# Four f tiles instead of six in the first phase of a fused attention and feed-forward kernel, with all later weights converted beside the attention

## The chip, the cores and the metric

The kernel runs on one core of one Trainium2 chip. The metric is the device time of one execution in microseconds (us). Engines are called as the profile calls them: PE is TensorE, DVE is VectorE, ACT is ScalarE, POOL is GpSimd, and SP is SyncE, whose queue issues nearly all DMAs.

## What is computed

Block-causal attention over 8 batches of 8 heads, 576 positions and 64 channels each, and on its output, as 4608 tokens of 512 channels, a feed-forward layer of width 2048 with a leaky activation:

```python
scores = scale * np.matmul(q, k.transpose(0, 1, 3, 2))        # (8, 8, 576, 576)
mask = block_i >= block_j                                     # blocks of 64
scores = np.where(mask, scores, -1000000000.0)
attn = np.exp(scores - np.max(scores, axis=-1, keepdims=True))
attn = attn / (np.sum(attn, axis=-1, keepdims=True) + 1e-09)
out = np.matmul(attn, v)
...
x = np.ascontiguousarray(attn_out.transpose(0, 2, 1, 3)).reshape(B * S, H * D)
h = x @ w_in                                                  # (4608, 512) x (512, 2048)
g = np.maximum(h, 0.0) + alpha * np.minimum(h, 0.0)
return (g @ w_out).astype(np.float32)                         # (2048, 512)
```

q, k and v are float32; the two weight matrices come as 64-bit floats, so that a half of an f tile's weights (its part of `w_in` or of `w_out`, 512 values per partition) arrives as 1024 words of 32 bits, and the kernel makes float32 of it.

## The kernel before

**Precision.** Products of float32 values are made of pairs: a value is split into a high part (rounded to the matmul's format by ACT) and a low part (the difference, by POOL or DVE; `split`, L526). A product is then three matmuls: high by high, high by low, low by high.

**Attention.** Two heads make a pair; there are 32 pairs, four to a batch. `prep` (L771) loads q, k and v of a pair, splits q and k, and moves the parts through 10 DMAs into the tiles `Q` and `K`. `query_tile` (L863) makes scores of 128 queries on PE (L890, L952), the negative maximum on DVE (L897, L903), the exponential with its sum on ACT (L906), sums and reciprocal on DVE (L910, L912), the scaling on POOL (L914), transposes on PE (L922, L978), and copies them from PSUM to `PTF` on ACT or DVE (L996, L998). `values` (L1000) multiplies with v (L1022); ACT copies the result into `xT` (L1026), a ring of two batches, and `spill` (L1032) stores each batch to `xd` in DRAM.

**Feed-forward, first phase.** The 2048 columns are 16 f tiles of 128. Tiles 0 to `FA` - 1 (six) are computed beside the attention, in 18 chunks of 256 tokens (`chunk_a`, L739): `split_x` makes `xh` and `xl`, `ffn1` (L615) is 12 matmuls of 256 columns per f tile (L623), `activate` (L631) works on ACT (L634, L640), DVE (L636) and POOL (L643), and `ffn2` (L647) adds three matmuls of 512 columns per f tile and 128 tokens (L660). The sum over these tiles goes to `part` in DRAM. The chunks fill PE between the attention's products.

**Feed-forward, later phase.** Once attention has ended its buffers are freed (`end_attention`, L1074), and the other ten f tiles are taken two by two over nine chunks of 512 tokens, with Strassen's scheme in Winograd's form for the first product: seven products of half size (`pair1`, L690; six matmuls of 256 columns each, L701) instead of eight. For that, sums of quarters of the weights (`ws`, L545) and of the tokens (`xt`, L545) are made and split (`w`, `X`, L529). DVE adds up the products (L710, L714). `store_out` (L1109) adds `part` and stores.

**Weights.** `to_f32` (L493) converts a half: one load of 512 KB on SP's queue into one of two `raw` buffers, then DVE (L507), ACT (L510) and DVE four times (L512, L516, L519, L522), with two PSUM banks. The 12 halves of the first phase are converted at the start. Of the 20 later halves, the four in `AHEAD` are converted during attention and stored to `wd` in DRAM (`weights_ahead`, L550), to be loaded back afterwards; the `w_in` halves of f tiles 6 and 7 are converted late in the attention, the other 14 behind it, beside the last chunks of the first phase and the first later chunk.

**What sets the order.** All steps are handed to a planner (`Plan`, L135) as operations with an engine, a cost, dependences, buffers and a priority. `schedule` (L180) plays them through with an event queue: each engine that is free takes the ready operation of the smallest priority whose buffers are to be had, and the instructions are issued in that order. On the chip each engine, SP's queue included, then runs its list in order. Attention of pair p has priority 5p and a little more; first-phase chunks have that of a pair `LAG` (6.75) pairs later than their tokens (`turn`, L598); `weights_ahead` has 5p + 100, so it takes what the others leave. `SHIFTS` adds numbers to single priorities (463 entries).

Of the kernel before, what the change touches and what calls it, by code (L numbers as in the profile page):

```python
# [9 lines left out]
F32 = mybir.dt.float32  # L10
F32R = mybir.dt.float32r
BF16 = mybir.dt.bfloat16
I32 = mybir.dt.int32
U32 = mybir.dt.uint32
AF = mybir.ActivationFunctionType
ALU = mybir.AluOpType
# [3 lines left out]
B, H, S, D = 8, 8, 576, 64  # L20
# [4 lines left out]
NCC = DM // P  # L25
NF = DF // P
TOK = B * S
FA = 6
# [13 lines left out]
LAG = 6.75  # L42
# [5 lines left out]
XP = 2.0  # L48
VAL = 1.5
CHANGE = 300  # L50
ON_DVE, D0 = (3,), 8
AHEAD = {(8 + k // 2, k % 2): 12 + 4 * k for k in range(4)}
SHIFTS = {
# [1117 lines left out]
```

## Time and profile before

| | before |
|---|---|
| median of 3 runs | 1110.31 us (1109.41 to 1111.34) |
| the profiled execution's own time | 1114.08 us |
| its span | 1112.3 us |
| PE, DVE, ACT, POOL busy | 98%, 63%, 56%, 54% |
| mean granted PE clock | 0.998 |
| DMA | 147.9 MB, 133 GB/s over the span |

The span is what the profiler recorded on the core; 1.8 us of the execution's own time lie around it. A row of busy times by stage reads: stage, its length, then for PE, PE's weight loads, DVE, ACT and POOL the busy us (with the number of instructions), then the granted clock of PE, the mean busy share of the 16 DMA engines, and GB/s. A row of the groups reads: line, engine, operation, written tile, read tiles, shapes and count, then busy us and mean ns of one, then idle us of the engine just before them with what ended it. Matmuls overlap, so the mean of one matmul is longer than the time that each takes up in a row of them; the chain of work shows the latter.

### The profile page before, as it was taken

To read this page: it belongs to the slowest core of one execution; us is meant where nothing else is said; L and a number is where in the kernel's file an instruction comes from. 1 tells how busy PE (TensorE), PEld (TensorE's weight loads), DVE (VectorE), ACT (ScalarE), POOL (GpSimd) and SP (SyncE) were. 2 spreads that over 40 slices of the span, in tenths; PEclk is the share of its full clock that TensorE was granted. 3 is DMA by queue.
4 is the path that set the end of the run, shared out by engine and by line. 5 is a ranking of instruction groups with operands and counts; after the bars stand their busy time and mean duration, and the time that the engine had idled before them with its cause. 6 is when DMAs were issued, how large, how long until landed. Compare 5 with 4: busy or idle time off the path is not lost.

```text
span 1112.3 us, 21554 instructions
## 1 busy us (share of the span) xinstructions
PE 1091.3 (98%) x7342; PEld 949.8 (85%) x7342; DVE 700.1 (63%) x1651; ACT 627.4 (56%) x1740; POOL 600.2 (54%) x771
## 2 busy tenths in 40 slices
PE   7989999999999999999999999999999999999998
PEld 5668888888888888888888888889898989898987
DVE  7787666565565655756548997564747555555554
ACT  7878877675676676757655655343433434343432
POOL 5657657655656555555569985343434435252522
PEclk9999999999999999999999999999999999999999
DMA  7897787766476774738343523130303030312021
GB/s 219 239 260 226 198 244 187 208 186 183 127 203 189 192 209 124 230 103 244 80 148 114 165 90 103 43 114 1 115 1 114 1 114 7 108 39 77 1 76 39
DMA packets 75309, 147.92 MB, mean 133 GB/s; under 512 B 9792, under 2 KB 11840, under 8 KB 75200
## 3 DMA queue, kind: packets, MB, share of 16 engines
q1 hardware_dynamic: 74768, 146.28, 44.9%
q8 instruction: 58, 0.95, 0.4%
q14 instruction: 51, 0.42, 0.1%
q10 hardware_dynamic: 432, 0.27, 0.1%
HBM read 68.40 MB, written 29.36 MB: 88 GB/s over the span
## 4 chain that ended last, share of the span: by engine, by line
PE 89%; DVE 3%; DMA 3%; POOL 2%; issue 1%; SPq 1%; ACT 0%; DVEq 0%; POOLq 0%
PE bank L660 34%; PE bank L701 20%; PE bank L623 12%; PE bank L1022 7%; PE bank L890 6%; PE bank L922 6%; DMA raw<-in_w_in 2%; PE bank L952 2%; PE bank L978 1%; DVE m L507 1%; DMA raw<-in_w_out 1%; POOL xl L611 0%; POOL w L529 0%; DVE m L519 0%; DVE bank L512 0%
## 5 line engine op out<-in xcount | busy, mean ns | idle before, releaser
L643 POOL TENSOR_TENSOR gl<-g,gh 128x256 fp32r<-128x256 f32 x288 | 220.9, 776 | 303.7 <-ACT gh L640 159.3
L701 PEld LDWEIGHTS bank<-X,w 128*128 128x128 f32 x1890 | 246.1, 189 | 16.6 <-DVE X L529 1.2
L701 PE MATMUL bank<-X,w 128*128 128x256 f32 x1890 | 250.7, 281 | 1.1 <-DVE X L529 1.0
L660 PE MATMUL bank<-w,gh 128*128 128x512 f32 x720 | 225.3, 394 | 0.0
L634 ACT ACTIVATE g<-bank 128x256 f32<-128x256 f32 x288 | 109.5, 384 | 197.2 <-DVE bank L714 164.0
L914 POOL TENSOR_SCALAR p<-p,ri 128x128 f32<-128x128 f32 (+3 forms) x256 | 137.6, 552 | 126.7 <-DVE ri L912 56.4
L636 DVE SCALAR_TENSOR_TENSOR g<-g,oal,bank 128x256 f32<-128x256 f32 x288 | 134.3, 476 | 57.9 <-ACT g L634 55.3
L640 ACT CAST gh<-g 128x256 fp32r<-128x256 f32 x288 | 116.4, 407 | 89.7 <-DVE g L636 85.5
L906 ACT ACTIVATE p<-bank,nm 128x256 f32<-128x256 f32 (+3 forms) x256 | 133.8, 530 | 34.9 <-DVE nm L903 15.5
L660 PE MATMUL bank<-w,gl 128*128 128x512 f32 x360 | 141.6, 393 | 0.0
L714 DVE TENSOR_TENSOR bank<-bank,g 128x256 f32<-128x256 f32 x180 | 75.0, 428 | 102.7 <-PE bank L701 99.0
L660 PE MATMUL bank<-wa,gh 128*128 128x512 f32 x432 | 139.6, 404 | 0.0
L660 PEld LDWEIGHTS bank<-w,gh 128*128 128x128 f32 x720 | 124.0, 188 | 17.4
L623 PE MATMUL bank<-xh,wa 128*128 128x256 f32 x864 | 128.1, 287 | 0.9 <-DVE PTF L996 0.7
L623 PEld LDWEIGHTS bank<-xh,wa 128*128 128x128 f32 x864 | 113.8, 190 | 4.5 <-DVE PTF L996 1.1
L922 PE MATMUL bank<-ident,p 128*128 128x128 f32 x640 | 100.6, 278 | 9.3 <-POOL p L914 7.4
L890 PE MATMUL bank<-K,Q 128*128 128x512 f32 (+1 forms) x472 | 100.1, 332 | 0.8 <-DMA K<-KL 0.7
L922 PEld LDWEIGHTS bank<-ident,p 128*128 128x128 f32 x640 | 76.0, 142 | 21.6 <-POOL p L914 12.1
L710 DVE TENSOR_TENSOR g<-bank,g 128x256 f32<-128x256 f32 x135 | 56.6, 421 | 59.6 <-PE bank L701 58.4
L1022 PE MATMUL bank<-PTF,vraw 128*64 128x320 f32 (+3 forms) x768 | 94.1, 384 | 0.0
L903 DVE TENSOR_REDUCE nm<-bank 128x1 f32<-128x512 f32 (+1 forms) x128 | 76.4, 617 | 23.0 <-PE bank L890 19.0
L660 PE MATMUL bank<-wa,gl 128*128 128x512 f32 x216 | 85.5, 396 | 0.5 <-POOL gl L643 0.4
(111 smaller groups left out, 1677.8 us busy)
## 6 DMA issues: line engine op xcount, KB each, us to landing
Q<-QH SPq DMA_DIRECT2D x62, 256.0 KB, 3.8
K<-KH SPq DMA_DIRECT2D x124, 128.0 KB, 3.7
vraw<-in_v SPq DMA_DIRECT2D x32, 320.0 KB, 4.2
qraw<-in_q SPq DMA_DIRECT2D x31, 320.0 KB, 3.8
xd<-xT SPq DMA_DIRECT2D x8, 1152.0 KB, 6.7
part<-o SPq DMA_DIRECT2D x36, 256.0 KB, 3.0
xb<-xd SPq DMA_DIRECT2D x9, 1024.0 KB, 5.4
m<-part SPq DMA_DIRECT2D x36, 256.0 KB, 2.9
```

Of the source, the lines that this page charges most:

```text
L623: nc.tensor.matmul(hp()[:, :n], ww()[:, 0, cc * P:(cc + 1) * P], x()[:, cc, :n], start=(i == 0 and cc == 0), stop=(i == 2 and cc == NCC - 1))
L634: op("ACT", c_act(CHA), lambda: nc.scalar.activation(out=g(), in_=hp()[:, ts], func=AF.Relu, scale=-1.0), r=[hp], w=[g], prio=FP)
L636: op("DVE", c_dve(CHA) + 60, lambda: nc.vector.scalar_tensor_tensor(out=g(), in0=g(), scalar=oal[:, f:f + 1], in1=hp()[:, ts], op0=ALU.mul ...
L640: op("ACT", c_act(CHA, True), lambda: nc.scalar.copy(out=gh(), in_=g()), r=[g], w=[gh], prio=FP)
L643: op("POOL", c_pool(CHA), lambda: nc.gpsimd.tensor_tensor(out=gl(), in0=g(), in1=gh().bitcast(F32), op=ALU.subtract), r=[g, gh], w=[gl], p ...
L660: nc.tensor.matmul(acc(), a()[:, ts], ww(), start=(first and i == 0), stop=(last and i == 2))
L701: nc.tensor.matmul(bank()[:, :CHA], W()[:, i, 256 * at + P * c:256 * at + P * c + P], B()[:, j, CHA * c:CHA * c + CHA], start=(n == 0), st ...
L890: nc.tensor.matmul(o, Q()[:, i, qs], K()[:, 2 * h + i, :w], start=(i == 0), stop=(i == 1))
L906: op("ACT", 238 + w / 1.2, lambda h=h, t=t: nc.scalar.activation(out=t()[:, :w], in_=sb[h]()[:, off[h]:off[h] + w], func=AF.Exp, bias=nm() ...
L914: op("POOL", 244 + w / 1.2, lambda h=h: nc.gpsimd.tensor_scalar(out=pts[h]()[:, :w], in0=pts[h]()[:, :w], scalar1=ri()[:, h:h + 1], scalar ...
L922: nc.tensor.transpose(out=tp()[:, base + c * P:base + (c + 1) * P], in_=pts[h]()[:, c * P:(c + 1) * P], identity=ident)
L1022: nc.tensor.matmul(ob()[rows[h], a - q0:q1 - q0], V()[:, c, h, :], moving, start=(c == 0), stop=(c == cs[-1][0]))
```

## The change

- `FA` is 4: the first phase computes f tiles 0 to 3, and the later phase tiles 4 to 15, as six pairs instead of five.
- `AHEAD` holds all 24 later halves, one per pair from pair 7 to pair 30. Nothing is converted behind the attention: the later phase only loads `wd` back.
- The sums of weight quarters and the low parts of the later weights, all on POOL before, are shared out by `ON`: the four sums, the second and the last of the four splits of W1, and the split of every first W2 of a pair on DVE, the others on POOL.
- The sums of weight quarters are kept in `m` tiles; `ws` is gone. `raw` lies among the attention's buffers, `o` among the first phase's. Of the buffers opened behind the attention there are now four W1, eight W2 and three X, and behind the first phase two, four and four (before 3, 6, 3 and 2, 4, 5).
- `LAG` is 6, `D0` is 4 (from pair 4 on instead of pair 8, two copies of a pair's probabilities are DVE's instead of ACT's), and `SHIFTS` has other entries, 36 of them.

```diff
-FA = 6
+FA = 4
...
-LAG = 6.75
+LAG = 6
...
+ON = ("DVE", "POOL", "DVE", "POOL", "DVE", "DVE", "POOL")
+W1B, W2B, XF, XW = 2, 4, 4, 3
...
-ON_DVE, D0 = (3,), 8
-AHEAD = {(8 + k // 2, k % 2): 12 + 4 * k for k in range(4)}
+ON_DVE, D0 = (3,), 4
+AHEAD = {(FA + k // 2, k % 2): 7 + k for k in range(2 * (NF - FA))}
 SHIFTS = {
-    -11: 1.5, -6: -0.5, -4.5: 1.3, -4: -3, -3.5: -6.1, 0: 2.2, 0.5: 0.1, 1: 2.7, 2: 3.4, 4.5: -1.2, 9: 2.6, 10: 1.7, 10.5: -0.8, 11: -0.8,
...
+    27: 3.7, 43.3333: 2.6, 49: -1.2, 53.8889: 2, 59: 1.4, 60.5: -1.9, 61.1111: -2, 61.6667: -4.9, 62.2222: -2.3, 65.5556: 1.9, 67: -1.3,
...
-    rooms(wraw, ("raw", RB, [1024], I32), ("m", EB, [512], F32))
-    rooms(st, ("qraw", 1, [QP], F32), ("kraw", 1, [S], F32), ("vraw", 1, [5, 2, D], F32), ("p", PB, [512], F32), ("pl", 1, [S], F32),
+    rooms(wraw, ("m", EB, [512], F32))
+    rooms(st, ("raw", RB, [1024], I32), ("qraw", 1, [QP], F32), ("kraw", 1, [S], F32), ("vraw", 1, [5, 2, D], F32), ("p", PB, [512], F32), ("pl", 1, [S], F32),
...
-          ("gl", GB, [CHA], F32R), ("o", 2, [DO], F32))
+          ("gl", GB, [CHA], F32R))
+    rooms(xring, ("o", 2, [DO], F32))
...
-            sb = Buf("ws")
+            sb = Buf("m")
...
-            add("POOL", 256, s1, q21, q22, ALU.add, pr, [m1, "att"])
-            add("POOL", 256, s2, s1, q11, ALU.subtract, pr)
-            add("POOL", 256, q21, q11, q21, ALU.subtract, pr)
-            for src, r, at, n, on in ((w0, [m0, "att"], 0, 512, "POOL"), (w1, [m1, q21[0]], 2, 512, "POOL"),
-                                      (lambda sb=sb: sb(), [s1[0], s2[0]], 4, 512, "POOL")):
+            add(ON[0], 256, s1, q21, q22, ALU.add, pr, [m1, "att"])
+            add(ON[0], 256, s2, s1, q11, ALU.subtract, pr)
+            add(ON[0], 256, q21, q11, q21, ALU.subtract, pr)
+            for src, r, at, n, on in ((w0, [m0, "att"], 0, 512, ON[1]), (w1, [m1, q21[0]], 2, 512, ON[2]),
+                                      (lambda sb=sb: sb(), [s1[0], s2[0]], 4, 512, ON[3])):
...
-            add("POOL", 256, s2, q12, s2, ALU.subtract, pr)
+            add(ON[0], 256, s2, q12, s2, ALU.subtract, pr)
...
-            split(s2[1], hi, lo, 256, [s2[0]], (("w1", f, 6), "h"), (("w1", f, 6), "l"), [W], "POOL", pr)
+            split(s2[1], hi, lo, 256, [s2[0]], (("w1", f, 6), "h"), (("w1", f, 6), "l"), [W], ON[4], pr)
...
-                split(w, hi, lo, 512, [mb], (("w", f + i, 1), "h"), (("w", f + i, 1), "l"), [W], "POOL", prio(f) + .5)
+                split(w, hi, lo, 512, [mb], (("w", f + i, 1), "h"), (("w", f + i, 1), "l"), [W], ON[5 + i], prio(f) + .5)
...
-        rooms("wb", ("w1", 3, [2, 7 * 256], F32R), ("w2", 6, [2, 512], F32R), ("xb", 1, [NCC, CHB], F32), ("X", 3, [2, 512], F32R),
-              ("m", 2, [512], F32), ("ws", 1, [512], F32), ("xt", 2, [512], F32), ("g", 4, [CHA], F32))
+        rooms("wb", ("w1", 6 - W1B, [2, 7 * 256], F32R), ("w2", 12 - W2B, [2, 512], F32R), ("xb", 1, [NCC, CHB], F32), ("X", XW, [2, 512], F32R),
+              ("m", 2, [512], F32), ("xt", 2, [512], F32), ("g", 4, [CHA], F32))
...
-        rooms("fx", ("w1", 2, [2, 7 * 256], F32R), ("w2", 4, [2, 512], F32R), ("X", 5, [2, 512], F32R),
+        rooms("fx", ("w1", W1B, [2, 7 * 256], F32R), ("w2", W2B, [2, 512], F32R), ("X", XF, [2, 512], F32R),
```

The lines of the changed kernel stand some 41 lower numbers: what is L636, L903, L996 and L1022 before is L595, L862, L955 and L981 after; L660 and L701 become L619 and L660.

50 rows, old and new, of the table SHIFTS are left out of this document.

## The prediction

> **What bounds the kernel now.** I read the busy times first, then the busy times by stage, then the chain of work that ended last, then the costliest groups and the waits of TensorE. From the page's first part:
>
> ```profile
> PE 1091.3 (98%) x7342; PEld 949.8 (85%) x7342; DVE 700.1 (63%) x1651; ACT 627.4 (56%) x1740; POOL 600.2 (54%) x771
> ```
>
> PE is busy for all but 21.0 of 1112.3 us. The busy times by stage say where those 21 us lie, and how full the other engines are beside it (columns: stage, PE, weight loads, DVE, ACT, POOL, granted clock, DMA share, GB/s):
>
> ```profile
> 0.00:100.00 100.00, 84.21 (x540) 63.62 (x541) 81.33 (x210) 77.19 (x213) 62.58 (x91) 0.98 0.83 238
> 30.00:100.00 70.00, 61.07 (x418) 47.89 (x415) 58.05 (x141) 55.53 (x152) 44.95 (x53) 0.98 0.86 245
> 80.00:90.00 10.00, 7.06 (x47) 5.93 (x43) 7.86 (x20) 6.34 (x18) 5.42 (x8) 0.83 0.84 223
> 100.00:200.00 100.00, 100.00 (x758) 85.11 (x756) 62.37 (x173) 77.05 (x235) 64.59 (x93) 1.00 0.78 214
> 200.00:500.00 300.00, 300.00 (x2181) 260.63 (x2179) 181.65 (x471) 196.70 (x590) 169.17 (x237) 1.00 0.62 176
> 600.00:690.00 90.00, 88.45 (x554) 78.28 (x554) 77.03 (x145) 54.23 (x124) 79.34 (x82) 1.00 0.36 112
> 650.00:680.00 30.00, 30.00 (x187) 26.72 (x186) 27.29 (x54) 17.37 (x39) 25.49 (x27) 1.00 0.23 71
> 690.00:1090.00 400.00, 400.00 (x2511) 360.07 (x2510) 228.94 (x498) 156.00 (x390) 155.53 (x180) 1.00 0.18 59
> 1090.00:1113.00 23.00, 18.63 (x103) 15.73 (x101) 8.94 (x20) 5.05 (x13) 4.34 (x7) 1.00 0.12 46
> ```
>
> 15.8 us of idle PE are in the first 100 us, 1.6 at the passage from attention to the later chunks, 4.4 at the end. In between PE is full, so what counts is how much work PE gets and whether the others can still feed it. The chain shows what PE's pieces cost back to back (start, us, matmuls), and two loads of raw weights on the early chain:
>
> ```profile
> 45.20 9.67 DMA raw<-in_w_in
> 72.26 10.62 DMA raw<-in_w_in
> 95.09 2.86 PE bank L1022 x28
> 573.48 6.99 PE bank L660 x30
> 580.47 8.41 PE bank L623 x70
> 1066.50 4.26 PE bank L701 x36
> ```
>
> So a 256-column matmul takes 0.120 us in the first phase (L623) and 0.118 us in a later product (L701); a 512-column one takes 0.233 us (L660).
>
> **PE's own work.** The counts:
>
> ```profile
> L701 PE MATMUL bank<-X,w 128*128 128x256 f32 x1890 | 250.7, 281 | 1.1 <-DVE X L529 1.0
> L623 PE MATMUL bank<-xh,wa 128*128 128x256 f32 x864 | 128.1, 287 | 0.9 <-DVE PTF L996 0.7 <-POOL wa L529 0.2
> L623 PE MATMUL bank<-xl,wa 128*128 128x256 f32 x432 | 70.8, 286 | 0.0
> ```
>
> The first phase spends 1296 matmuls on six f tiles, 216 each. The later phase takes two tiles as a pair in 378 (1890 / 5 pairs), where the first phase takes 432. The change moves one pair: 432 x 0.120 = 51.9 us leave, 378 x 0.118 = 44.7 us come. That is **-7 us**, with nothing beside it to hide it, as PE is full. Second products are as many as before (three of 512 columns per f tile and 128 tokens, in either phase).
>
> **The start.** PE loses 15.8 us there. 12 halves of first weights become 8, so four conversions leave the first 100 us. One conversion is five operations on DVE and one on ACT:
>
> ```profile
> L507 DVE TENSOR_SCALAR m<-raw 128x512 int32<-128x512 int32 x32 | 23.7, 740 | 8.7 <-POOL m L545 4.5 <-DMA raw<-in_w_in 2.3 <-DMA raw<-in_w_out 1.7
> L510 ACT ACTIVATE bank<-m,ebias 128x512 int32<-128x512 int32 x32 | 22.3, 696 | 10.8 <-DVE m L507 10.7
> L512 DVE SCALAR_TENSOR_TENSOR bank<-raw,bank 128x512 int32<-128x512 int32 x32 | 21.9, 689 | 3.3 <-ACT bank L510 2.8
> L516 DVE TENSOR_SCALAR bank<-raw 128x512 int32<-128x512 int32 x32 | 21.9, 683 | 6.0 <-DMA raw<-in_w_in 3.9 <-DMA raw<-in_w_out 2.1
> L522 DVE SCALAR_TENSOR_TENSOR m<-m,bank 128x512 f32<-128x512 f32 x32 | 21.6, 681 | 0.2
> L519 DVE SCALAR_TENSOR_TENSOR m<-raw,bank 128x512 f32<-128x512 uint32 x32 | 21.6, 680 | 0.0
> ```
>
> 0.740 + 0.689 + 0.683 + 0.681 + 0.680 = 3.47 us of DVE each, 13.9 us for four, of DVE's 81.3 in that stage; and four loads of 512 KB fewer, of the kind that took 9.7 and 10.6 us on the chain. Against that, `D0` hands two copies of four early pairs from ACT to DVE:
>
> ```profile
> L996 DVE COPY PTF<-bank 128x512 f32<-128x512 f32 x80 | 53.5, 687 | 47.0 <-PE bank L978 26.1 <-PE bank L922 20.6
> ```
>
> 8 x 0.687 = 5.5 us of DVE, mostly after the stage's worst part. And the two chunks that fill PE's gaps early shrink by two f tiles each: 4 x (12 x 0.120 + 6 x 0.233 = 2.84) = 11.4 us less filler. Bounds: -10 (the idle time after 30 us, 70.0 - 61.1 = 8.9, and the clock's dip) to +4 (a third of the missing filler shows as idle). I take **-4**, nearer the gain because DVE waits for those loads with attention queued behind it. The row of 80 to 90 us has 2.9 us of idle PE and a clock of 0.83, so an early stall costs more than its own length. The Trainium skill, "TensorE: Matmul & The Clock Gate", section "What's actually happening", puts the array at half clock after an idle window of some 3.4 us; the trace agrees in kind, with a shorter gap than that on record here, and by the page a stall under the window would cost its length alone.
>
> **The middle of attention.** 24 conversions, one per pair from pair 7 on, replace six there. Each brings a 512 KB load and a 256 KB store. They are put where DVE has room by their late priority, but DVE and the SP queue run in order. On DVE, at a pair in the last third of the attention, stand before:
>
> ```order
> L996 COPY PTF_104<-bank_143 128x4x2x64
> L903 TENSOR_REDUCE nm_197<-bank_212 128x1
> L903 TENSOR_REDUCE nm_197<-bank_254 128x1
> L903 TENSOR_REDUCE nm_192<-bank_229 128x1
> L910 TENSOR_REDUCE sp_278<-s_137 128x2
> L903 TENSOR_REDUCE nm_192<-bank_182 128x1
> L912 RECIPROCAL ri_294<-sp_278 128x2
> L910 TENSOR_REDUCE sp_208<-s_135 128x2
> L912 RECIPROCAL ri_222<-sp_208 128x2
> L636 SCALAR_TENSOR_TENSOR g_533<-g_533,oal,bank_189 128x256
> ```
>
> and now, at a like place (L466, L471 and L478 are steps of a conversion, `raw` its input; L595, L862 to L871 and L955 are the former L636, L903 to L912 and L996):
>
> ```order
> L466 TENSOR_SCALAR m_327<-raw_258 128x512
> L869 TENSOR_REDUCE sp_213<-s_135 128x2
> L871 RECIPROCAL ri_256<-sp_213 128x2
> L869 TENSOR_REDUCE sp_287<-s_133 128x2
> L871 RECIPROCAL ri_238<-sp_287 128x2
> L471 SCALAR_TENSOR_TENSOR bank_143<-raw_258,bank_143 128x512
> L955 COPY PTF_105<-bank_223 128x4x2x64
> L955 COPY PTF_105<-bank_249 128x4x128
> L955 COPY PTF_105<-bank_189 128x4x128
> L568 CAST xh_451<-xT 128x512 x2
> L478 SCALAR_TENSOR_TENSOR m_327<-raw_258,bank_233 128x512
> ```
>
> The steps of a conversion now stand between the sums (`sp`), the copies of the probabilities (`PTF`) and the factors of a chunk, each of which PE waits for. On the SP queue at a like place, first before, then now:
>
> ```order
> L776 DMA qraw_226<-in_q 128x640
> L777 DMA kraw_232<-in_k 128x576
> L778 DMA vraw_168<-in_v 128x640
> L791 DMA Q_127<-QH_292 64x2x512 x2
> L791 DMA K_129<-KH_301 64x512 x2
> ```
>
> ```order
> L735 DMA qraw_236<-in_q 128x640
> L515 DMA wd<-m_229 128x512
> L464 DMA raw_258<-in_w_out 128x1024
> L750 DMA K_129<-KH_317 64x512 x4
> L750 DMA K_129<-KL_339 64x512 x2
> ```
>
> A store that waits for the last step of a conversion (`wd`), and a load that waits for a raw buffer, now stand ahead of a pair's moves of K; if DVE is late, that pair's scores are late with it. Rows for the balance, of the stage from 200 to 500 us where it is so named (L1022, L623 and L512 there), else of the whole run:
>
> ```profile
> 200.00:500.00 300.00, 43.92 (x420) 1.00 0.62 176
> ...
> 200.00:500.00 300.00, 94.57 (x698) 1.00 0.62 176
> ...
> L512 DVE SCALAR_TENSOR_TENSOR bank<-raw,bank 128x512 int32<-128x512 int32 x6 | 4.1, 691 | 0.6 <-ACT bank L510 0.5
> ```
>
> ```profile
> L636 DVE SCALAR_TENSOR_TENSOR g<-g,oal,bank 128x256 f32<-128x256 f32 x288 | 134.3, 476 | 57.9 <-ACT g L634 55.3
> L640 ACT CAST gh<-g 128x256 fp32r<-128x256 f32 x288 | 116.4, 407 | 89.7 <-DVE g L636 85.5 <-PE bank L660 2.2
> L634 ACT ACTIVATE g<-bank 128x256 f32<-128x256 f32 x288 | 109.5, 384 | 197.2 <-DVE bank L714 164.0 <-PE bank L623 28.2 <-POOL w L529 1.4
> ```
>
> ```profile
> raw<-in_w_in SPq DMA_DIRECT2D x16, 512.0 KB, 5.6
> ...
> wd<-m SPq DMA_DIRECT2D x4, 256.0 KB, 2.9
> ```
>
> These 300 us hold 420 / 28 = 15 pairs, 698 / 12 = 58 activations and six conversions. With four f tiles for six, 19.4 activations go, and 19.4 x 2.84 = 55 us of PE: 245 us for the same pairs. DVE there: 181.7 - 19.4 x 0.476 + 9 x 3.47 = 203.7 us, **83%** of 245 (61% before). ACT: 196.7 - 19.4 x 0.791 + 9 x 0.696 = 187.6, 77%. DMA: 176 GB/s x 300 us = 52.8 MB, plus 9 x 0.768 = 59.7 MB, 244 GB/s, and a share of 0.62 x 300 x 59.7 / 52.8 / 245 = **0.86**. That is the mix of the row from 30 to 100 us (DVE 83%, ACT 79%, DMA 0.86), in which PE was busy for 87%; the row from 100 to 200 us (62%, 77%, 0.78) kept PE full. 25 pairs from pair 7 on take 25 x 245 / 15 = 408 us, so each per cent of PE lost costs 4 us. Bounds: 0 (as from 100 to 200 us) to +61 (408 / 0.87 - 408). I take **+4**, near the lower end, since the early row's shortage had causes that are absent here: first weights needed at once, and hardly any chunk ready to fill gaps.
>
> **The passage.** What PE has left behind the last pair's values shrinks from 228 first and 141 second matmuls to 144 and 75, 60 us to 34.8 us of cover. But no raw weights are left to convert in it, only `wd` to load back and to combine. The combining moves from POOL to DVE in most parts. POOL before, at the first later pair:
>
> ```order
> L545 TENSOR_TENSOR ws_6515<-ws_6515,m_323 128x256
> L545 TENSOR_TENSOR m_203<-m_323,m_203 128x256
> L529 TENSOR_TENSOR w_6513<-ws_6515,w_6513 128x512
> L529 TENSOR_TENSOR w_6513<-m_203,w_6513 128x512
> L545 TENSOR_TENSOR ws_6515<-m_323,ws_6515 128x256
> ```
>
> DVE now, at the first later pair (L504 and L488 are the former L545 and L529):
>
> ```order
> L504 TENSOR_TENSOR m_6097<-m_6097,m_327 128x256
> L504 TENSOR_TENSOR m_6011<-m_327,m_6011 128x256
> L488 TENSOR_TENSOR w_6014<-m_6011,w_6014 128x512
> L504 TENSOR_TENSOR m_6097<-m_327,m_6097 128x256
> L504 TENSOR_TENSOR xt_6147<-xb_6026 128x512
> L488 TENSOR_TENSOR w_6014<-m_6097,w_6014 128x256
> L595 SCALAR_TENSOR_TENSOR g_6155<-g_6155,oal,bank_249 128x256
> ```
>
> The four sums and three of six splits of a pair are on DVE now, ahead of an activation (L595) for which PE's second products wait. Nearest rows, the last from the stage 600 to 690 us alone:
>
> ```profile
> L529 DVE TENSOR_TENSOR X<-xt,X 128x512 fp32r<-128x512 f32 x18 | 20.8, 1161 | 0.0
> L714 DVE TENSOR_TENSOR bank<-bank,g 128x256 f32<-128x256 f32 x180 | 75.0, 428 | 102.7 <-PE bank L701 99.0 <-ACT gh L640 1.7 <-ACT g L634 0.6
> L529 DVE TENSOR_TENSOR X<-xb,X 128x512 fp32r<-128x512 f32 x9 | 7.0, 781 | 0.0
> ...
> L529 DVE TENSOR_TENSOR X<-xt,X 128x512 fp32r<-128x512 f32 x3 | 4.3, 1449 | 0.0
> ```
>
> Per pair two 512-wide and five 256-wide operations: 2 x 0.78 + 5 x 0.43 = 3.7 us at best, 2 x 1.45 + 5 x 0.8 (an estimate: somewhat over half of 1.45) = 6.9 at worst; six pairs 22 to 41 us. From the last values to the end of the first later chunk PE has 34.8 + 6 x (42 x 0.118 + 24 x 0.233 = 10.55) = 98 us. DVE's other work in it is about 0.572 x 63.3 = 36 us (the row from 690 to 1090 us: 228.9 / 400) plus two last conversions 6.9, 12 activations 5.7 and the first factors 3.1: 52. Together 74 to 93 of 98 us. The row from 650 to 680 us has DVE at 91% with PE full. So **+1**, bounds -2 (the 1.6 us of now go) to +8 (DVE late by the difference of the two prices for two or three pairs). The Trainium skill, "GPSIMD Engine Reference", section "1. Specifications", says that POOL's SBUF interfaces are shared with VectorE, with contention for DVE instructions with two SBUF inputs. That speaks against moving these sums beside POOL's own subtractions; the trace agrees, as the same split took 1.45 us in the stage with POOL at 88% and 1.16 over the run.
>
> **Edits at nothing.** In the steady later chunks DVE is at 57% and PE full. Seven X buffers instead of eight: each is released by the last pair's product and wanted again six products and the second products between later, about 10 us, against some 2 us to refill; without that cover each of eight chunk edges would pay up to 2 us. The last 4.4 us stay. LAG and the new shifts only set the order, costed above.
>
> **Sum.** -7 - 4 + 4 + 1 = -6 us. The profiled execution's own time is 1114.1 us (span 1112.3), 3.8 above the median of 1110.3; -6 on it is 1108.1, on the median **1104.3 us**, 0.5% faster. About 0.2% (2.2 us) is what a measurement of this kernel can tell from no change.
>
> **Rivals.** (1) DVE in order becomes the bound of the attention: a conversion step or a late `wd` store ahead of K's moves starves PE. It decides from 2.5% of PE lost (10 us) and, at 5%, costs 20: -7 - 4 + 20 + 1 = +10, **1120 us**. For it: 83% of DVE, DMA 0.86, and this wait of the SP queue for conversions:
>
> ```profile
> SPq L505 <- DVE m L519: 53.4, 13, 10.1
> ```
>
> Against it: six conversions from 200 to 500 us left PE full. Chance 0.27. (2) The passage pays the worst DVE price, by the shared interface, +6: -7 - 4 + 4 + 6 = -1, **1109**, no change. Chance 0.14. (3) The start gains all 10 and attention stays full: -7 - 10 + 1 = -16, **1094**. For it, the DMA loads of 10 us on the early chain; against it, less filler. Chance 0.14. The forecast, PE's saving with small changes around it, 1098 to 1108: 0.45.
>
> So faster 0.45 + 0.14 = 0.59, same 0.14, slower 0.27. The range reaches from just under (3), 1093, to 1122, past (1) at 5%; what is left out is mainly attention losing more than 5.5%.
>
> **What would show it.** Right: 864 first matmuls in the first phase and 2268 later ones; PE full by stage from about 90 us on; DVE at 80 to 87% in mid-attention; first later product some 35 to 38 us behind the last values. Wrong: PE under 97% in mid-attention, with its scores waiting for moves of K, or its transposes for POOL behind DVE's sums; DVE over 95% in the first later chunk with PE waiting for `w` or `X`; or idle time in the first 100 us unchanged or larger.

## The result, and the profile after

The changed kernel takes **1121.1 us** (median of 4 runs, 1118.06 to 1121.97) against 1110.6 for the kernel before on the same chip: a ratio of 1.0091 [1.007, 1.0112], 0.9% slower, 10.1 us. The forecast was 1104.3, with slower at 0.27. The profiled execution took 1120.97 us, its span is 1119.2 and its mean granted clock 0.995 (before: 1114.08, 1112.3, 0.998).

The instructions are those that were forecast. Of the groups of the kernel after (L660 is the later product, the former L701; L582 is `ffn1`, the former L623):

```profile
L660 PE MATMUL bank<-X,w 128*128 128x256 f32 x2268 | 312.4, 282 | 5.6 <-ACT X L487 5.4
L582 PE MATMUL bank<-xh,wa 128*128 128x256 f32 x576 | 88.3, 287 | 1.6 <-DVE xh L568 1.0 <-ACT pl L924 0.5
L582 PE MATMUL bank<-xl,wa 128*128 128x256 f32 x288 | 48.0, 289 | 0.0
```

2268 later matmuls and 864 first ones. The first row has what is new, an idle 5.4 us of PE for one X. The busy times by stage of the kernel after (columns as before the change; ten-us rows at the passage):

```profile
PE 1094.4 (98%) x7288; PEld 944.4 (84%) x7288; DVE 753.3 (67%) x1764; ACT 625.2 (56%) x1743; POOL 579.3 (52%) x735
```

```profile
0.00:100.00 100.00, 89.86 (x571) 67.35 (x572) 75.64 (x207) 75.47 (x215) 64.96 (x96) 0.98 0.90 239
80.00:90.00 10.00, 9.97 (x74) 9.12 (x73) 8.93 (x23) 8.27 (x25) 8.45 (x12) 1.00 1.00 304
100.00:200.00 100.00, 99.74 (x744) 83.20 (x742) 79.73 (x210) 79.64 (x247) 65.68 (x93) 1.00 0.91 256
200.00:490.00 290.00, 287.74 (x2143) 244.21 (x2143) 229.15 (x584) 217.12 (x658) 186.81 (x258) 1.00 0.85 241
500.00:600.00 100.00, 91.53 (x560) 79.67 (x559) 80.37 (x134) 54.44 (x127) 69.30 (x62) 0.97 0.38 119
530.00:540.00 10.00, 7.63 (x39) 5.94 (x39) 5.60 (x9) 5.26 (x12) 6.17 (x6) 1.00 0.41 136
540.00:550.00 10.00, 6.08 (x29) 5.26 (x30) 5.59 (x11) 5.64 (x13) 6.16 (x5) 0.66 0.40 117
690.00:1090.00 400.00, 400.00 (x2501) 359.30 (x2501) 219.31 (x480) 152.47 (x384) 149.49 (x176) 1.00 0.13 46
```

Three things are to be seen. In the first 100 us PE idles for 10.1 us instead of 15.8 (how much of this is the change's comes below). From 100 to 490 us it is at 99% and more, though DVE is now at 79% (229.15 / 290) and DMA at 0.85: close to the forecast's 83% and 0.86. And the passage, 500 to 600 us, has 8.5 us of idle PE and a clock of 0.97, in two slices above all. The waits of that stretch (engine and line, what it waited for: us, times, longest):

```profile
PE bank L660 <- ACT X L487: 5.4, 1, 5.4
ACT X L487 <- DMA part<-o: 5.0, 1, 5.0
```

A cast of an X, which reads tokens, waits for the **store of a first-phase sum**. The chain of waits shows how (start, us, what):

```profile
529.72 4.07 DMA m<-wd
...
534.54 1.41 DVE m L504
...
538.97 0.37 SPq L521
...
539.39 3.62 DMA part<-o
543.01 0.02 issue
543.03 0.04 ACTq L487
543.07 0.04 issue
543.11 0.63 ACT X L487
543.74 0.07 issue
543.81 1.29 POOL X L488
545.10 0.04 issue
545.14 2.09 PE bank L660 x8
```

and so does SP's queue (the instructions in order of time):

```profile
538.55 0.80 SPq L521 DMA_DIRECT2D m<-wd  x2
539.39 0.59 SPq L723 DMA_DIRECT2D part<-o  x1
```

The change puts the two `o` tiles into the first phase's pool. The buffers of X numbers four to seven, opened when that pool closes, lie where it was. So the fourth X waits until the last `part<-o` has landed, and that store is queued on SP behind loads of `wd`, which wait for `m` buffers and so for DVE's splits and sums (L488, L504). The queue is the smaller part: the last copies into `o`, on ACT behind a cast of `w` that waited 2.17 us for DVE's sums, end only at 538.09 us,

```profile
537.02 1.07 ACT L722 COPY o<-bank 128x512 f32<-128x512 f32 x2
```

so a free queue would have brought the store forward by 1.3 us (an estimate, 539.39 - 538.09). The rest is the store's own 3.62 us and the cast of X behind it. PE, with three products done, stands:

```profile
536.02 2.31 PE L660 MATMUL bank<-X,w 128*128 128x256 f32 x18
543.78 5.18 PE L660 MATMUL bank<-X,w 128*128 128x256 f32 x24 [5.45 <-ACT X L487]
```

The 24 matmuls behind the gap take 5.18 us instead of 24 x 0.118 = 2.8: the clock of that slice is 0.66. So the one wait costs 5.45 + 2.35, nearly 8 us, in this execution.

### The profile page after: what moved, and what is told of

It reads as the page before. It is cut to its first block, busy times and chain, and to the rows that moved or that the text cites. A ratio compares the mean times of both kernels' runs of the same rounds, so it can differ in the third digit from the quotient of the medians.

```text
span 1119.2 us, 21769 instructions
## 1 busy us (share of the span) xinstructions
PE 1094.4 (98%) x7288; PEld 944.4 (84%) x7288; DVE 753.3 (67%) x1764; ACT 625.2 (56%) x1743; POOL 579.3 (52%) x735
## 4 chain that ended last, share of the span: by engine, by line
PE 88%; DVE 3%; DMA 3%; POOL 2%; ACT 2%; issue 1%; SPq 0%; DVEq 0%; ACTq 0%; POOLq 0%
PE bank L619 33%; PE bank L660 23%; PE bank L981 8%; PE bank L582 7%; PE bank L849 6%; PE bank L881 6%; PE bank L911 2%; PE bank L937 1%; DVE m L504 1%; POOL p L873 1%; DMA qraw<-in_q 1%; PE bank L844 1%; DMA K<-KL 1%; DMA o<-in_k 0%; ACT p L865 0%
## 5 line engine op out<-in xcount | busy, mean ns | idle before, releaser
L660 PEld LDWEIGHTS bank<-X,w 128*128 128x128 f32 x2268 | 306.4, 190 | 29.0 <-ACT X L487 5.7
L660 PE MATMUL bank<-X,w 128*128 128x256 f32 x2268 | 312.4, 282 | 5.6 <-ACT X L487 5.4
L619 PE MATMUL bank<-w,gh 128*128 128x512 f32 x864 | 271.5, 395 | 0.0
L873 POOL TENSOR_SCALAR p<-p,ri 128x384 f32<-128x384 f32 (+3 forms) x256 | 148.2, 594 | 84.2 <-DVE ri L871 56.5
L619 PE MATMUL bank<-w,gl 128*128 128x512 f32 x432 | 170.1, 394 | 0.7 <-POOL gl L602 0.7
L595 DVE SCALAR_TENSOR_TENSOR g<-g,oal,bank 128x256 f32<-128x256 f32 x288 | 136.2, 475 | 39.7 <-ACT g L593 32.8
L619 PEld LDWEIGHTS bank<-w,gh 128*128 128x128 f32 x864 | 144.4, 188 | 15.7 <-ACT gh L599 0.5
L865 ACT ACTIVATE p<-bank,nm 128x384 f32<-128x384 f32 (+3 forms) x256 | 134.2, 534 | 29.4 <-DVE nm L862 13.2
L619 PEld LDWEIGHTS bank<-w,gl 128*128 128x128 f32 x432 | 81.3, 188 | 21.2 <-POOL gl L602 2.1
L981 PE MATMUL bank<-PTF,vraw 128*64 128x320 f32 (+3 forms) x768 | 96.6, 387 | 1.0 <-ACT PTF L957 1.0
L619 PE MATMUL bank<-wa,gh 128*128 128x512 f32 x288 | 93.5, 406 | 1.0 <-ACT gh L599 1.0
L862 DVE TENSOR_REDUCE nm<-bank 128x1 f32<-128x384 f32 (+1 forms) x128 | 76.2, 616 | 21.3 <-PE bank L849 19.3
L582 PE MATMUL bank<-xh,wa 128*128 128x256 f32 x576 | 88.3, 287 | 1.6 <-DVE xh L568 1.0
L981 PEld LDWEIGHTS bank<-PTF,vraw 128*64 128x64 f32 x768 | 50.3, 138 | 40.1 <-ACT PTF L957 4.2
```

The lines of the kernel that those rows point to most:

```text
L582: nc.tensor.matmul(hp()[:, :n], ww()[:, 0, cc * P:(cc + 1) * P], x()[:, cc, :n], start=(i == 0 and cc == 0), stop=(i == 2 and cc == NCC - 1))
L595: op("DVE", c_dve(CHA) + 60, lambda: nc.vector.scalar_tensor_tensor(out=g(), in0=g(), scalar=oal[:, f:f + 1], in1=hp()[:, ts], op0=ALU.mul ...
L619: nc.tensor.matmul(acc(), a()[:, ts], ww(), start=(first and i == 0), stop=(last and i == 2))
L660: nc.tensor.matmul(bank()[:, :CHA], W()[:, i, 256 * at + P * c:256 * at + P * c + P], B()[:, j, CHA * c:CHA * c + CHA], start=(n == 0), st ...
L865: op("ACT", 238 + w / 1.2, lambda h=h, t=t: nc.scalar.activation(out=t()[:, :w], in_=sb[h]()[:, off[h]:off[h] + w], func=AF.Exp, bias=nm() ...
L873: op("POOL", 244 + w / 1.2, lambda h=h: nc.gpsimd.tensor_scalar(out=pts[h]()[:, :w], in0=pts[h]()[:, :w], scalar1=ri()[:, h:h + 1], scalar ...
```

## The experiments

All times are medians; ratios are to the kernel before, run beside each, and 0.001 of ratio is 1.1 us. Leave-outs keep the order of all that is left.

**First question: is it the place of `o`, the crowded attention, or the order?** Four kernels.

`o_apart` gives `o` room that no later X lies on, and pays for it with one `g`, `gh` and `gl` less behind the first phase:

```diff
-    rooms(xring, ("o", 2, [DO], F32))
+    rooms(wraw, ("o", 2, [DO], F32))
...
-              ("g", 2, [CHA], F32), ("gh", 2, [CHA], F32R), ("gl", 2, [CHA], F32R))
+              ("g", 1, [CHA], F32), ("gh", 1, [CHA], F32R), ("gl", 1, [CHA], F32R))
```

> The changed kernel with the two o tiles out of the first phase's buffers, among those that stay to the end, so that the later X tiles' room no longer overlies them; to make room, the last buffers opened hold one g, gh and gl fewer each. Theory A (the fourth X waits for the last store of part, because its room overlies o): PE's 5.4 us wait at the fourth product shrinks to about 1 to 2 us, the clock dip behind it goes, the time falls by 5 to 8 us to about 1114. Rival B (the wait is DVE's lateness with the later weights, o only happened to come last): the wait stays at 4 us or more, time within 2 us of the changed kernel. In both the last pair's values end at about 497 us, unchanged.

Measured: **1115.25 us**, 1.0039 [1.0023, 1.0056]. The wait is gone, and what is left of it are short ones with the clock at full speed:

```profile
537.02 0.74 PE L660 MATMUL bank<-X,w 128*128 128x256 f32 x4 [0.29 <-ACT X L487]
538.40 2.68 PE L660 MATMUL bank<-X,w 128*128 128x256 f32 x18 [0.65 <-POOL X L488]
541.54 0.51 PE L660 MATMUL bank<-X,w 128*128 128x256 f32 x2 [0.46 <-POOL X L488]
```

So the place of `o` costs 0.0091 - 0.0039 = 0.0052, **5.8 us**. The kernel is still slower than before.

`no_arith` does not issue the DVE and ACT operations of the 24 conversions beside the attention, `no_load` does not issue their 24 loads of 512 KB; `o` stays as the change has it. Weights are then not the reference's. For `no_arith`, with the same for the other five operations (for `no_load`, on the load's `dma_start`):

```diff
-        op("DVE", c_dve2(512), lambda: nc.vector.tensor_scalar(
+        op("DVE", c_dve2(512), lambda: "arith" in left or nc.vector.tensor_scalar(
```

> The changed kernel with the same order, but the 24 conversions in mid-attention issue neither their five DVE operations nor the one on ACT; loads of raw weights and stores to wd stay, so the later weights hold stale numbers. Theory A (DVE in order starves PE in mid-attention): the last pair's values end 7 to 10 us earlier than the changed kernel's 497.5 us, time 1111 to 1114. Rival C (DMA traffic or the SP queue does it): they end within 2 us of 497.5, time within 3 us of 1121. Rival D (the order of the work itself is worse than before's, not its resources): also within 2 us.

> The changed kernel with the same order, but without the 24 loads of raw weights (512 KB each) in mid-attention; the conversions work on stale words, the stores to wd stay, so the later weights hold stale numbers. Theory A (DVE): last values within 2 us of 497.5. Rival C (DMA share of 0.9): last values 5 to 9 us earlier, time 1112 to 1116. Rival D (order): within 2 us.

Measured: 1118.63 us, 1.0071 [1.0052, 1.009], and 1118.32, 1.0072 [1.0044, 1.01]: 2 us each, inside the intervals of the kernel after. The wait for X stays (5.2 and 5.8 us). In the profiled executions the values (L981) take 481.1 and 481.0 us from the first to the last, as in the kernel after (481.0), so neither half alone shows a gain in the attention. Crowding is not the main cost.

`before_plain` is the kernel before with no shifts:

```diff
-SHIFTS = {
...
-}
+SHIFTS = {}
```

> The kernel before with no SHIFTS at all, all else as before. Rival D (the 463 shifts of before had been worth several us, and the change gives them up for 36): 1117 to 1135 us. Theory A (resources, not order): 1109 to 1114 us.

Measured: 1125.84 us, 1.0135 [1.0107, 1.0164]. Its 463 shifts are worth 15 us to the kernel before. That made a second theory worth testing: the change throws this order away, and that is the rest of the loss.

**Second question: is the rest the order?** Four kernels.

`before_o_over` puts the fault into the kernel before, `o` under the later X:

```diff
-          ("gl", GB, [CHA], F32R), ("o", 2, [DO], F32))
+          ("gl", GB, [CHA], F32R))
+    rooms(xring, ("o", 2, [DO], F32))
```

> The kernel before, with one edit: the two o tiles stand in the pool of the later first weights, under the later X tiles, as the change has them; order and all else as before. Theory A (the later X wait for the last store of a part of the output): PE waits 4 to 6 us for X at the first later products, about 543 us in the kernel after and about 640 us here, and the time is 1115 to 1117 us. Rival D (what the change lost is its coarser order, not the place of o): 1111 us, with no such wait.

Measured: 1116.42 us, 1.0048 [1.0033, 1.0063]: +5.3 us, the same price from the other side. The wait and PE there (L529 and L702 are the former L528 and L701):

```profile
ACT X L529 <- DMA part<-o: 3.0, 1, 3.0
```

```profile
629.18 2.31 PE L702 MATMUL bank<-X,w 128*128 128x256 f32 x18
633.69 3.01 PE L702 MATMUL bank<-X,w 128*128 128x256 f32 x10 [2.20 <-ACT X L529]
637.02 3.36 PE L702 MATMUL bank<-X,w 128*128 128x256 f32 x14 [0.33 <-DVE X L530]
```

The wait is 2.2 us, shorter than expected; the 24 matmuls behind it take 6.37 us instead of 2.8, and these make the rest.

`o_apart_plain` is `o_apart` with `SHIFTS = {}`.

> The changed kernel with the o tiles apart from the later X and with no shifts at all, to be set beside the kernel before with no shifts (1125.8 us). Theory (PE's saving of 7 us is real, and what is lacking is the order): 1117 to 1121 us, 5 to 8 under that kernel. Rival E (four f tiles cost at the start, in the attention and in the passage what they save): 1124 us or more.

Measured: 1114.22 us, 1.0027 [1.0014, 1.0039]. Without shifts the change (with `o` apart) is 0.0108 of ratio, 12 us, *faster* than the kernel before without shifts, more than expected; and its own 36 shifts bring nothing that can be told (1.0039 with them).

`tuned` and, later, `tuned2` are `o_apart` with two other sets of 786 and 793 shifts.

> The changed kernel with o apart (1115.3 us) and with several hundred small shifts of the order's keys, as many as the kernel before has, instead of the 40 of the change. Theory D (the order is what is lacking): 1103 to 1108 us, below the kernel before. Rival (four f tiles leave PE the same waits in any order): 1112 to 1116 us.

> The changed kernel with o apart (1115.3 us) and another set of several hundred small shifts, nearer to the order that it has. Theory D (a finer order brings what the kernel before gains by its own shifts): 1108 us or less. Rival (of the order, little is to be had by such shifts, since what is left is in the passage): 1112 to 1117 us.

Measured: 1117.83 us, 1.0057 [1.0035, 1.0079], and 1114.43, 1.0036 [1.0023, 1.0048]. Neither gains; the first is slower than both of its expectations. The theory that a finer order is what is lacking is not borne out: two fine orders and none at all lie within 3.6 us. Shifts fitted in another way could still do better; that stays open.

**Third question: the engines that combine the later weights.** `on_pool` is `o_apart` with that work on POOL alone, as before the change:

```diff
-ON = ("DVE", "POOL", "DVE", "POOL", "DVE", "DVE", "POOL")
+ON = ("POOL",) * 7
```

> The changed kernel with o apart (1115.3 us), with all later weights combined on POOL instead of mostly on DVE. Rival 2 of the prediction (the sums on DVE, two SBUF inputs beside POOL, are what the passage pays for): 1110 to 1113 us. Theory (DVE's slow sums cost 2 us at most, and POOL alone is the slower engine for this work): 1117 to 1128 us, with PE waiting for w or X from POOL in the first later chunks.

Measured: 1125.72 us, 1.0134 [1.0114, 1.0154], 10 us slower than `o_apart`. The stage from 496 to 590 us, first of `on_pool`, then of `o_apart`:

```profile
496.00:590.00 94.00, 83.25 (x494) 72.04 (x491) 40.95 (x80) 48.43 (x112) 85.72 (x90) 0.95 0.35 117
```

```profile
496.00:590.00 94.00, 89.54 (x554) 77.44 (x555) 76.54 (x129) 53.23 (x127) 67.59 (x60) 1.00 0.41 131
```

POOL is at 91% and PE does 494 matmuls instead of 554; from 490 to 600 us PE waits 7.0 us for `w` (4.3 for POOL, 2.7 for ACT). DVE is the better place; but with it PE still idles 4.5 us. It does not wait for the combined weights there. All its waits in `o_apart` from 490 to 600 us:

```profile
PE bank L660 <- POOL X L488: 1.1, 2, 0.6
PE bank L619 <- ACT gh L599: 1.0, 2, 0.7
PE bank L582 <- DVE xh L568: 1.0, 2, 0.6
PE bank L619 <- POOL gl L602: 0.8, 2, 0.7
PE bank L660 <- ACT X L487: 0.3, 1, 0.3
```

They are for parts of the tokens (`xh`, `X`) and of the activations (`gh`, `gl`), which DVE, ACT and POOL make between the weights' steps.

`no_sums` is `o_apart` less the combining of the later weights: the sums and the low halves (DVE and POOL) and the high halves of the sums (ACT) are not issued, and PE reads loaded parts in their place, in as many matmuls. `before_no_sums` is the kernel before with the same left out. The edits in both (besides, the ACT cast and the read of W2's low half, likewise):

```diff
+LEFT = ("later weights",)
...
-        op(e, c_pool(n) if e == "POOL" else c_dve(n), lambda: (nc.gpsimd if e == "POOL" else nc.vector).tensor_tensor(
+        op(e, c_pool(n) if e == "POOL" else c_dve(n), lambda: (n == 256 and "later weights" in LEFT) or (nc.gpsimd if e == "POOL" else nc.vector).tensor_tensor(
...
-                        nc.tensor.matmul(bank()[:, :CHA], W()[:, i, 256 * at + P * c:256 * at + P * c + P], B()[:, j, CHA * c:CHA * c + CHA],
+                        nc.tensor.matmul(bank()[:, :CHA], W()[:, 0, 256 * (at % 4) + P * c:256 * (at % 4) + P * c + P], B()[:, j, CHA * c:CHA * c + CHA],
```

> The changed kernel with o apart (1115.3 us), less the combining of the later weights: their sums and the low halves of their splits (DVE and POOL), and ACT's high halves of the sums, are not issued, and TensorE reads loaded parts in their place, as many matmuls as before; the order stays. Theory E (the passage pays some 4 us because DVE, POOL and ACT share these sums): 1109 to 1112 us, with the first to the last product in 564.7 us or less and under 1 us of idle PE in the first later chunk. Rival (the passage costs what it did, and the loss lies in the start and in the attention): 1114 to 1116 us.

> The kernel before with the same left out as in the run without the later weights' sums and low halves (there 106.9 above the thousand, 8.4 us less than with them); the order stays. Theory E (that price is what the change brought by putting these sums on DVE beside fuller engines): 1108 to 1111 us, 0 to 3 less than the kernel before. Rival (the sums cost about the same in the kernel before, where POOL makes them): 1102 to 1105 us.

Measured: `no_sums` 1106.86 us, 0.9968 [0.995, 0.9986]; `before_no_sums` 1109.24, 0.9993 [0.9981, 1.0005]. The combining costs 0.0071, **7.9 us**, in the changed kernel, more than the theory's 4 us, and 0.0007, 0.8 us, in the kernel before, which its interval does not tell from nothing. The same stage of `no_sums`, and the passages of the kernel before with and without the combining, each from the end of its last values (571.2 and 566.7 us):

```profile
496.00:590.00 94.00, 92.75 (x603) 83.28 (x599) 47.81 (x96) 51.92 (x122) 42.26 (x47) 1.00 0.39 134
```

```profile
571.20:690.00 118.80, 117.25 (x728) 103.95 (x729) 98.62 (x176) 68.68 (x156) 104.64 (x107) 1.00 0.42 135
```

```profile
566.70:685.50 118.80, 117.68 (x735) 104.94 (x736) 92.57 (x178) 65.27 (x147) 53.05 (x57) 1.00 0.42 136
```

Without the combining PE does 603 matmuls in these 94 us instead of 554 (`o_apart`), and its waits from 490 to 600 us are 0.9 us for `X` and 0.4 for `xh`. In the kernel before it does 735 instead of 728 in 118.8 us: there the combining was nearly hidden.

`lean` is `o_apart` less both the loads and the operations of the 24 conversions (`left=("arith", "load")`); their stores stay, of data that is not the weights.

> The changed kernel with o apart (1115.3 us), less both the loads and the DVE and ACT operations of the 24 conversions beside the attention (their stores stay, of data that is not the weights); the order stays. Rival 1 of the prediction (the crowded attention costs 10 us or more): 1105 us or less. The prediction's own +4: 1111. Theory (DVE in order and the queues have room, crowding costs 0 to 2 us): 1113 to 1115 us, with the last values 0 to 2 us earlier, counted from the first.

Measured: 1111.06 us, 1.0002 [0.9989, 1.0016]: crowding costs 0.0037, **4.1 us**, about the sum of the two halves' 2 us. From 200 to 490 us, `lean` and then `o_apart`:

```profile
200.00:490.00 290.00, 288.57 (x2142) 245.97 (x2140) 177.18 (x492) 207.15 (x638) 182.50 (x258) 1.00 0.72 204
```

```profile
200.00:490.00 290.00, 287.73 (x2143) 244.77 (x2140) 229.90 (x586) 216.88 (x658) 185.13 (x257) 1.00 0.84 239
```

With DVE at 61% instead of 79% PE does as many matmuls in this stage, and the 4 us hardly show as idle PE. Most of them lie in the attention all the same. The values, in `lean` and then in `o_apart` (first and last start):

```profile
L981 PE MATMUL bank<-PTF,vraw x768: 272/432/796, 14.3 to 492.4; 128*64 128x320 f32 x96, 128*64 128x256 f32 x32, 128*64 128x128 f32 x32, 128*64 128x192 f32 x32
L981 PE MATMUL bank<-PTF,vraw x768: 272/432/797, 14.8 to 495.6; 128*64 128x320 f32 x96, 128*64 128x256 f32 x32, 128*64 128x128 f32 x32, 128*64 128x192 f32 x32
```

They take 478.1 us instead of 480.8, and the first later product starts 38.5 us behind their end in both (531.2 and 534.4 us). So 2.7 us are lost beside the conversions, in one execution of each; what holds PE up there is not settled.

No kernel of these computes the reference and beats the kernel before.

## Why the prediction was wrong, point by point

The forecast was 6 us faster, the change is 10.1 us slower. The runs give a sum of their own: place of `o` +5.8, combining in the passage 7.9 - 0.8 = +7.1, crowding +4.1, together +17.0; measured +10.1. The rest, **-6.9**, is what PE's saving and the start bring together. (The three prices come from different kernels, each with its interval of some 2 us, and the kernel before has a few conversions beside the attention too, so this is good to about 3 us. `no_sums` and `before_no_sums`, 2.8 us apart, give the same -6.9 once the crowding is taken off; that is the same sum in another order, not a second measurement.)

- **PE's own work, -7: right, by counts and prices.** The counts are as forecast, and so are the prices: on the chain of the kernel after 48 matmuls of L582 take 5.77 us, 0.120 each, and six of L660 0.71 us, 0.118 each. No run measured the saving by itself.
- **The start, -4: not found.** If PE's work brings -7, the rest of -6.9 leaves the start about 0. The -4 was read from one execution, which took 3.8 us more than its kernel's median. `before_o_over` has the same instructions in the same order as the kernel before, with only `o` placed elsewhere, and its first 100 us are:

```profile
0.00:100.00 100.00, 88.21 (x570) 68.74 (x571) 84.33 (x218) 79.82 (x221) 67.12 (x96) 0.97 0.86 246
```

  PE idles for 11.8 us there, not 15.8, and no load of raw weights is on the chain of these 100 us. So of the 5.7 us of idle time that went from the kernel before to the kernel after some 4 are a difference between executions, and the loads of 10 us on the early chain were no fixed cost of that kernel. The clock's dip at 80 to 90 us has moved, not gone: the kernel after has a clock of 0.69 from 60 to 65 us. No run measured the start alone.
- **The middle of attention, +4: right**, DVE 79% against 83%, DMA 0.85 against 0.86, price 4.1. Rival 1, PE starved by DVE or SP's queue in the attention, did not happen; that the time is nearly the 1120 us that it gave is chance.
- **The passage, +1: the step that failed.** The prediction set DVE's load, 74 to 93 us, against PE's 98 us and saw that it fits. It does fit: DVE has 76.5 us of 94 in `o_apart`. The step from there to +1 failed: the combining cost the change 7.1 us although none of the engines that do it was full. With it, PE waits 4.2 us in `o_apart` from 490 to 600 us, without it (`no_sums`) 1.3, and never for `w`. What fits this is that steps for tokens and activations stand behind the weights' steps on DVE, ACT and POOL, while the cover on PE, from the last values to the first later product, has gone from 61.2 us to 38.5; no run tested another order of these steps. DVE's part of the combining, in the kernel after, 497 to 590 us:

```profile
L504 DVE TENSOR_TENSOR m<-m,m 128x256 f32<-128x256 f32 x18 | 15.5, 889 | 0.1
L504 DVE TENSOR_TENSOR m<-m 128x256 f32<-128x256 f32 x6 | 6.4, 1062 | 1.6 <-DMA m<-wd 1.6
L488 DVE TENSOR_TENSOR w<-m,w 128x512 fp32r<-128x512 f32 x12 | 13.5, 1128 | 3.3 <-ACT w L487 3.2
L488 DVE TENSOR_TENSOR w<-m,w 128x256 fp32r<-128x256 f32 x6 | 3.9, 648 | 0.1
```

  The sums take 0.89 and 1.06 us, above the prediction's worst price of 0.8 (at best 0.43), the wide splits 1.13 (0.78 to 1.45). Together they are 39.3 us, inside the predicted 22 to 41: the load was sized right, at its upper end. Rival 2 had the right stage and nearly its price (+6 for 7.1, which is also inside the bound of +8), but its cause, DVE slowed by POOL on the shared interface, is not shown: no run took POOL's work alone away.
- **"Edits at nothing": the step that was not seen.** The rearranged tiles were priced by the number of X buffers alone. That `o` moved under X makes a wait out of a store that nobody waited for before: +5.8, shown from both sides.
- **LAG and the new shifts, "only set the order": half right.** The changed kernel's time hardly hangs on the shifts (with `o` apart 1.0039, 1.0027, 1.0057 and 1.0036; no run changed `LAG` alone), but the 463 shifts that went were worth 15 us to the kernel before. Judged without shifts the change would have been 12 us faster with `o` apart. Why the changed kernel, without any, stands so much better than the kernel before without any is open.

The right sum of the prediction's own terms is thus -7 + 0 + 4 + 7, and +6 for the place of `o`: +10. None of the signs that it named for being wrong would have shown this: PE stayed at 99% in mid-attention, DVE was at 78% (76.09 of 98 us) from 497.5 to 595.5 us in the kernel after, and idle time in the first 100 us fell.

## What to carry to other kernels

When tiles move between pools, ask for each buffer that is opened later whose last reader it must wait for, and where that reader stands on its queue: a store that nobody needs can end up ahead of the first product. A passage between two phases is not judged by the balance of its busy times: here the added work cost 7 us on engines that all had room. Ask what else stands behind the new work on each engine, and how much cover the bound engine has left. Before a term is read from one execution, ask how far that execution lies from the median. And a change to a kernel with a fitted order is best compared at equal fitting as well, for the order's worth can be larger than the change's.

## What the runs showed of the hardware

A gap of 2.2 us on PE was followed by 24 matmuls in 6.37 us instead of 2.8 (`before_o_over`); one of 5.45 us by 24 in 5.18 us (kernel after). The slice of 10 us held a granted clock of 0.66 in the kernel after and, in `before_o_over`, of 0.67:

```profile
630.00:640.00 10.00, 7.33 (x37) 6.54 (x36) 7.16 (x14) 5.85 (x15) 6.92 (x6) 0.67 0.58 191
```

So the length of the gap does not set the price alone. Rows of 1 and 2 us show what differs. In `before_o_over` the clock falls to 0.50 some 2.0 us into the gap, at about 633.5 us (0.75 in the row of 633 to 634), just before PE starts again; in the kernel after 2.7 us into it, at about 541.0 (0.75 in the row of 540 to 542), so that some 2.8 us of the slow stretch pass while PE stands. The stretch is as long in both: 8 us around it have a mean clock of 0.57, which is 6.9 us at 0.50. The Trainium skill, "TensorE: Matmul & The Clock Gate", section "What's actually happening", names an idle window of some 3.4 us for half clock; a gap below it was enough here, as the prediction's row of 80 to 90 us had suggested. In `on_pool` the row of 556 to 557 us has a clock of 0.57, behind gaps of 1.45 and 0.26 us.
